# One of eight score slots per head moved from TensorE to VectorE and ScalarE in a decode attention kernel, with another slot map for the last head

## The chip, the cores and the metric

One core of one Trainium2 chip. The metric is the device time of one execution in microseconds (us).

## The reference, cut to what matters

Two attention blocks (A and B) for one query token, 32 heads each, 8192 cached keys and values of 128 numbers in bf16. The kernel walks through the 64 heads one after the other.

```python
q = (x @ wq).reshape(B, Sq, H, Dh).transpose(0, 2, 1, 3)          # 1 token, 32 heads
scores = jnp.einsum("bhqd,bhkd->bhqk", q, k_cache) * (Dh ** -0.5)  # 8192 scores per head
p = softmax(scores, axis=-1)
o = jnp.einsum("bhqk,bhkd->bhqd", p, v_cache)
return o.transpose(0, 2, 1, 3).reshape(B, Sq, H * Dh) @ wo
```

## The kernel before

K of one head lies in SBUF as 128 partitions by 64 columns of 128 numbers; the 64 columns are cut into 8 *slots* g0 to g7 of 8 columns. A slot's scores come in one of two ways, by a letter in a map:

- "P": TensorE transposes the 8 blocks, ScalarE copies them to SBUF, TensorE multiplies them by q (one-column products), and one ScalarE copy brings the scores to `ssb`.
- "D": VectorE runs 8 fused multiplies with an accumulator, straight from K.

What follows the scores is the same for every head: the max reduce on VectorE and GpSimd's max over the partitions, the exp on ScalarE, GpSimd's sum over the partitions, and on TensorE the *PV products* (probabilities times V), the *selection* (which picks out and adds up the parts of their result), and, after VectorE's normalisation, the *projection* by `wo`.

The lines that matter, with cuts:

```python
NK, NV, NWO, QB0, VCH, MAP = 4, 4, 8, 8, 4, "PDPDPDDD"
...
# GpSimd, for every head n
def armax(n):
    W(pl, s_rmx, n + 1)                                  # after VectorE's max reduce
    pl.partition_all_reduce(gmx[:, n:n+1], mx[:, n:n+1], 128, ROP.max).then_inc(s_g1, 1)
    W(pl, s_g1, n + 1)
    pl.tensor_scalar(nb[:, n:n+1], gmx[:, n:n+1], -scale, None, AluOpType.mult).then_inc(s_nbr, 1)
def aradd(n):
    W(pl, s_expd, n + 1)                                 # after ScalarE's exp
    pl.partition_all_reduce(gs[:, n:n+1], rs[:, n:n+1], 128, ROP.add).then_inc(s_gsr, 1)
...
# SyncE: K of head n may be loaded when head n-4 has been read
W(sp, s_tf, NP * m); W(sp, s_sttd, ND * m)
sp.dma_start(kb[:, n % NK], kvw[b][:, h]).then_inc(s_kl[n % NK], 16)
...
# VectorE, one turn per slot t = 8 n + g, in this order:
#   g1: max reduce of head n-1    g4: normalisation of head n-2
#   g5: reciprocal of head n-1 (waits for GpSimd's sum gs)    then the slot's own 8 multiplies
ins = dve.scalar_tensor_tensor(junk[...], kb[:, n % NK, j, :], 1.0, qrep[:, n % 2, :],
        AluOpType.mult, AluOpType.mult, accum_out=ssb[:, n % 2, cm[j]:cm[j] + 1])
```

## Time and profile before

| | before |
|---|---|
| time, first three executions | 1574.52 us median (1568.42 to 1582.11) |
| VectorE / TensorE / ScalarE busy | 38% / 26% / 12% |
| share of the 16 transfer engines | 46% |
| steady period, max reduce to max reduce | 24.26 us |

No engine is near full. Here are lines of the page of the kernel before: span, busy us (share) per engine, the K and V queue's packets, MB and share of the span, the chain of waits that ended last by what held it, and groups with count, busy us, mean ns of one, then the idle time before them and what ended it.

```profile
span 1571.5 us, 17156 instructions
PE 416.0 (26%) x4736; PEld 248.4 (16%) x4736; DVE 598.2 (38%) x5383; ACT 185.8 (12%) x513; POOL 67.3 (4%) x198
...
q1 hardware_dynamic: 30196, 285.23, 46.0%
...
issue 70%; DVE 22%; POOL 4%; ACT 1%; DMA 1%; POOLq 1%; PE 0%; ACTq 0%; SPq 0%; DVEq 0%
...
L467 DVE TENSOR_SCALAR oT<-sb,rinv 128x1 bf16<-128x1 f32 x64 | 14.1, 221 | 670.3 <-PE sb L341 670.1
...
L375 ACT ACTIVATE psb<-ssb,nb 128x64 bf16<-128x64 f32 x64 | 22.2, 348 | 1195.6 <-POOL nb L213 1195.6
...
L461 DVE RECIPROCAL rinv<-gs 128x1 f32<-128x1 f32 x64 | 10.5, 164 | 279.9 <-POOL gs L217 279.9
L213 POOL TENSOR_SCALAR nb<-gmx 128x1 f32<-128x1 f32 x64 | 16.7, 260 | 725.3 <-issue 725.3
L217 POOL PARTITION_ALL_REDUCE gs<-rs x64 | 25.7, 402 | 391.1 <-issue 391.1
```

Look at the last two lines. GpSimd itself computes for 17 us and 26 us, but stands 725 and 391 us in front of these instructions with "issue" as the reason: nothing that the profile counts as a wait. That "issue" is 70% of the chain. ScalarE's exp waits 1196 us for the first of them.

The timeline of the kernel before, over one loop of the middle (start, duration, engine, instruction; idle time before in brackets; the VectorE multiplies are among the lines left out):

```profile
810.97 0.22 DVE L456 TENSOR_REDUCE mx<-ssb 128x1 f32<-128x64 f32 x1
811.01 0.33 SPq L153 DMA_DIRECT2D kb<-in_B_k_cache_dram  x1
...
811.29 0.38 POOL L211 PARTITION_ALL_REDUCE gmx<-mx  x1 [5.64 <-DVE mx L456]
811.38 0.43 SPq L166 DMA_DIRECT2D vb<-in_B_v_cache_dram  x1
...
822.33 0.26 POOL L213 TENSOR_SCALAR nb<-gmx 128x1 f32<-128x1 f32 x1 [10.67 <-issue]
822.63 0.35 ACT L375 ACTIVATE psb<-ssb,nb 128x64 bf16<-128x64 f32 x1 [18.27 <-POOL nb L213]
...
824.74 0.22 DVE L467 TENSOR_SCALAR oT<-sb,rinv 128x1 bf16<-128x1 f32 x1 [9.95 <-PE sb L341]
...
828.57 0.40 POOL L217 PARTITION_ALL_REDUCE gs<-rs  x1 [5.97 <-issue]
...
829.00 0.16 DVE L461 RECIPROCAL rinv<-gs 128x1 f32<-128x1 f32 x1 [4.04 <-POOL gs L217]
```

This is the loop that sets the time. Max reduce, then about 11 us until GpSimd's scaled maximum `nb`, then the exp, then about 6 us until GpSimd's sum `gs`, then VectorE's reciprocal; behind it, in VectorE's order, stand slots g5 to g7 and the next max reduce. I call the stretch from the end of the max reduce to the start of `nb` **the step**.

Two stretches of the kernel before, of about the same kind (the columns are the stretch and its length, busy us and instructions of PE, PEld, DVE, ACT and POOL, granted TensorE clock, transfer share, GB/s): the step of head 32, and that of head 62, near the end, when all K and V are loaded.

```profile
811.00:823.00 12.00, 0.00 (x0) 0.00 (x0) 3.79 (x34) 0.37 (x3) 0.64 (x2) 0.50 0.91 357
1533.70:1541.10 7.40, 0.00 (x0) 0.00 (x0) 3.43 (x32) 0.00 (x0) 0.38 (x1) 0.50 0.00 0
```

VectorE does about the same in both (3.79 and 3.43 us); the transfers run in one only, and the step is 4 to 5 us shorter without them.

### The profile page before, as it was taken

To read this page: it belongs to the slowest core of one execution; us is meant where nothing else is said; L and a number is where in the kernel's file an instruction comes from. 1 tells how busy PE (TensorE), PEld (TensorE's weight loads), DVE (VectorE), ACT (ScalarE), POOL (GpSimd) and SP (SyncE) were. 2 spreads that over 40 slices of the span, in tenths; PEclk is the share of its full clock that TensorE was granted. 3 is DMA by queue.
4 is the path that set the end of the run, shared out by engine and by line. 5 is a ranking of instruction groups with operands and counts; after the bars stand their busy time and mean duration, and the time that the engine had idled before them with its cause. 6 is when DMAs were issued, how large, how long until landed. Compare 5 with 4: busy or idle time off the path is not lost.

```text
span 1571.5 us, 17156 instructions
## 1 busy us (share of the span) xinstructions
PE 416.0 (26%) x4736; PEld 248.4 (16%) x4736; DVE 598.2 (38%) x5383; ACT 185.8 (12%) x513; POOL 67.3 (4%) x198
## 2 busy tenths in 40 slices
PE   2313133132231331322312223132232221331321
PEld 2101122121111110111111111011111110111110
DVE  3243342442433424424334243342442433424343
ACT  1101101011011010110110101011011010110110
POOL 0000000000000000000000000000000000000000
PEclk9955555555555555555555555555555555555555
DMA  9953544535435345354353443534535435345400
GB/s 380 424 216 131 221 158 175 217 127 209 179 153 220 152 180 217 123 213 172 160 221 143 188 191 140 220 133 199 198 140 215 178 154 221 135 197 209 158 22 0
DMA packets 30291, 286.32 MB, mean 182 GB/s; under 512 B 4210, under 2 KB 12404, under 8 KB 12916
## 3 DMA queue, kind: packets, MB, share of 16 engines
q1 hardware_dynamic: 30196, 285.23, 46.0%
q8 instruction: 38, 0.62, 0.2%
q14 instruction: 57, 0.47, 0.1%
HBM read 285.21 MB, written 0.00 MB: 181 GB/s over the span
## 4 chain that ended last, share of the span: by engine, by line
issue 70%; DVE 22%; POOL 4%; ACT 1%; DMA 1%; POOLq 1%; PE 0%; ACTq 0%; SPq 0%; DVEq 0%
DVE junk L440 21%; POOL gs L217 2%; POOL gmx L211 2%; POOL nb L213 1%; DVE mx L456 1%; ACT psb L375 1%; DMA wqs<-in_A_wq_dram 1%; DVE rinv L461 1%; POOLq L59 0%; POOLq L213 0%; PE qpb L229 0%; ACTq L123 0%; DVE osb L474 0%; SPq L144 0%; PE misc L354 0%
## 5 line engine op out<-in xcount | busy, mean ns | idle before, releaser
L440 DVE SCALAR_TENSOR_TENSOR junk<-kb,qrep 128x128 bf16<-128x128 bf16 x2560 | 557.7, 286 | 1.0 <-ACT qrep L368 0.8
L295 PE MATMUL sb<-qT,kt 128*128 128x1 bf16 x1536 | 73.9, 169 | 1093.0 <-ACT kt L392 1093.0
L467 DVE TENSOR_SCALAR oT<-sb,rinv 128x1 bf16<-128x1 f32 x64 | 14.1, 221 | 670.3 <-PE sb L341 670.1
L295 PEld LDWEIGHTS sb<-qT,kt 128*128 128x128 bf16 x1536 | 67.4, 109 | 1107.3 <-ACT kt L392 1107.0
L440 DVE DVE_READ_ACCUMULATOR junk<-kb,qrep 128x1 f32 x2560 | 209.4, 82 | 0.1
L279 PE MATMUL tb<-ident,kb 128*128 128x128 bf16 x1536 | 185.8, 297 | 2.2 <-DMA kb<-in_A_k_cache_dram 2.2
L375 ACT ACTIVATE psb<-ssb,nb 128x64 bf16<-128x64 f32 x64 | 22.2, 348 | 1195.6 <-POOL nb L213 1195.6
L279 PEld LDWEIGHTS tb<-ident,kb 128*128 128x128 bf16 x1536 | 139.6, 135 | 102.0 <-issue 99.6
L321 PE MATMUL db<-vb,psb 128*4 128x512 bf16 x1024 | 149.6, 574 | 16.7 <-ACT psb L375 16.7
L392 ACT ACTIVATE kt<-tb 128x512 f32<-128x512 f32 x192 | 113.2, 590 | 110.7 <-PE tb L279 110.7
L461 DVE RECIPROCAL rinv<-gs 128x1 f32<-128x1 f32 x64 | 10.5, 164 | 279.9 <-POOL gs L217 279.9
L213 POOL TENSOR_SCALAR nb<-gmx 128x1 f32<-128x1 f32 x64 | 16.7, 260 | 725.3 <-issue 725.3
L217 POOL PARTITION_ALL_REDUCE gs<-rs x64 | 25.7, 402 | 391.1 <-issue 391.1
L354 PE MATMUL misc<-wos,oT 128*1 128x512 bf16 x64 | 40.3, 630 | 2.8 <-DVE oT L467 2.8
L211 POOL PARTITION_ALL_REDUCE gmx<-mx x64 | 24.2, 379 | 375.8 <-DVE mx L456 375.8
L385 ACT ACTIVATE dsb<-db 128x512 bf16<-128x512 f32 x64 | 37.5, 586 | 2.2 <-PE db L321 2.2
L321 PEld LDWEIGHTS db<-vb,psb 128*4 128x4 bf16 x1024 | 23.3, 80 | 33.4 <-ACT psb L375 17.7
L368 ACT ACTIVATE qrep<-sb 128x128 bf16<-128x128 f32 x64 | 17.8, 278 | 69.6 <-PE sb L254 69.6
L254 PE MATMUL sb<-diag,ones 128*128 128x128 bf16 x64 | 16.9, 264 | 22.7 <-issue 22.0
L341 PE MATMUL sb<-sel,dsb 128*128 128x1 bf16 x256 | 17.0, 170 | 0.7 <-ACT dsb L385 0.7
L341 PEld LDWEIGHTS sb<-sel,dsb 128*128 128x128 bf16 x256 | 11.8, 107 | 29.2 <-ACT dsb L385 28.8
L423 DVE TENSOR_SCALAR diag<-ident,qT 128x128 bf16<-128x128 bf16 x64 | 16.0, 250 | 0.1
(20 smaller groups left out, 70.7 us busy)
## 6 DMA issues: line engine op xcount, KB each, us to landing
kb<-in_A_k_cache_dram SPq DMA_DIRECT2D x32, 2048.0 KB, 8.0
vb<-in_A_v_cache_dram SPq DMA_DIRECT2D x32, 2048.0 KB, 12.7
kb<-in_B_k_cache_dram SPq DMA_DIRECT2D x32, 2048.0 KB, 7.7
vb<-in_B_v_cache_dram SPq DMA_DIRECT2D x31, 2048.0 KB, 12.4
wqs<-in_A_wq_dram SPq DMA_DIRECT2D x1, 4096.0 KB, 13.2
wos<-in_A_wo_dram SPq DMA_DIRECT2D x32, 128.0 KB, 12.5
wqs<-in_B_wq_dram SPq DMA_DIRECT2D x1, 4096.0 KB, 42.6
wos<-in_B_wo_dram SPq DMA_DIRECT2D x32, 128.0 KB, 12.2
```

The costliest lines, as they stand in the source:

```text
L211: pl.partition_all_reduce(gmx[:, n:n + 1], mx[:, n:n + 1], 128, ROP.max).then_inc(s_g1, 1)
L213: pl.tensor_scalar(nb[:, n:n + 1], gmx[:, n:n + 1], -scale, None, AluOpType.mult).then_inc(s_nbr, 1)
L217: pl.partition_all_reduce(gs[:, n:n + 1], rs[:, n:n + 1], 128, ROP.add).then_inc(s_gsr, 1)
L279: ins = pe.transpose(tb[E % 2][:, i * 128:(i + 1) * 128], kb[:, n % NK, j, :], ident[:, :])
L295: ins = pe.matmul(sbk[n2 % 2][:, cm[j]:cm[j] + 1], kt[:, E % 2, i * 128:(i + 1) * 128], qT[:, n2:n2 + 1], start=True, stop=True,)
L321: ins = pe.matmul(dbk[n3 % 2][32 * c:32 * c + 4, 0:512], psb[:, n3 % 2, c0:c0 + 4], vb[:, n3 % NV, 4 * i:4 * i + 4, :].rearrange("p a d -> ...
L341: ins = pe.matmul(sbk[(n4 + 1) % 2][:, OC:OC + 1], dsb[:, n4 % 2, m * 128:(m + 1) * 128], sel[:, m:m + 1], start=(m == 0), stop=(m == 3),)
L354: pe.matmul(misc[0:1, 0:DO], oT[:, n5:n5 + 1], wos[:, n5 % NWO, :], start=(h == 0), stop=(h == H - 1),).then_inc(s_pjd, 1)
L375: act.activation(psb[:, n6 % 2, :], ssb[:, n6 % 2, :], AF.Exp, bias=nb[:, n6:n6 + 1], scale=scale, accum_out=rs[:, n6:n6 + 1],).then_inc(s ...
L385: act.activation(dsb[:, n7 % 2, :], dbk[n7 % 2][:, :], AF.Copy).then_inc(s_devd, 1)
L392: act.activation(kt[:, E % 2, :].bitcast(F32), tb[E % 2][:, :].bitcast(F32), AF.Copy,).then_inc(s_ev, 1)
L440: ins = dve.scalar_tensor_tensor(junk[:, (Sd % 2) * 8 + i, :], kb[:, n % NK, j, :], 1.0, qrep[:, n % 2, :], AluOpType.mult, AluOpType.mult ...
```

## The change

The intent: take one of three slots from TensorE (g4), give it to VectorE as one 128x1024 multiply with 8 accumulating copies on ScalarE behind it ("A"), and in the last head give more slots to TensorE, so that the end of the program is shorter. TensorE's selection and projection also move ahead of the PV products.

```diff
-    NK, NV, NWO, QB0, VCH, MAP = 4, 4, 8, 8, 4, "PDPDPDDD"
+    NK, NV, NWO, QB0, VCH = 4, 4, 8, 8, 4
+    MAP, MAPL, NLAST = "PDPDADDD", "PDPDPAPD", 1
 ...
+        junk2 = SB("junk2", [128, 8, 128], BF)
+        prod = SB("prod", [128, 2, 8, 128], BF)
 ...  (TensorE: the block of PV products now stands behind selection and projection)
 ...  (ScalarE)
+                if 0 <= n < N and g >= 1 and smap(n)[g - 1] == "A":
+                    W(act, s_pm, A + 1)
 ...
+                    for i in range(8):
+                        ins = act.activation(
+                            junk2[:, i, :], prod[:, A % 2, i, :], AF.Copy,
+                            accum_out=ssb[:, n % 2, cm[j]:cm[j] + 1],
+                        )
+                    ins.then_inc(s_aacc, 1)
 ...  (VectorE, max reduce)
+                    W(dve, s_aacc, cumA[n1 + 1])
 ...  (VectorE, slot "A")
+                    dve.tensor_tensor(
+                        prod[:, A % 2], kb[:, n % NK, 8 * g:8 * g + 8, :], qrep_b(n, 8), AluOpType.mult,
+                    ).then_inc(s_pm, 1)
```

(The rest of the diff counts semaphores per head, because the maps now differ between heads.)

More of the change, by code (lines that the diff above doesn't have):

```diff
@@ L37, in bass_concat_heads__mha_block_cached__gqa_block_cached__decode_kernel, with smap, slots, colmap @@
     assert DO <= 512 and N <= 64 and JT == 64 and NG == 8
-    assert len(MAP) == NG and set(MAP) <= set("PD")
-    pslots = [g for g in range(NG) if MAP[g] == "P"]
-    dslots = [g for g in range(NG) if MAP[g] == "D"]
-    NP = len(pslots)
-    ND = len(dslots)
-    assert pslots == [2 * i for i in range(NP)] and NP >= 1 and ND >= 1
-    cm = {}
-    for i, g in enumerate(pslots + dslots):
-        for r in range(8):
-            cm[8 * g + r] = 8 * i + r
+    assert len(MAP) == NG and len(MAPL) == NG
+    def smap(n):
+        return MAPL if n >= N - NLAST else MAP
+    def slots(n, kind):
+        return [g for g in range(NG) if smap(n)[g] == kind]
+    for m_ in (MAP, MAPL):
+        pl_ = [g for g in range(NG) if m_[g] == "P"]
+        assert pl_ == [2 * i for i in range(len(pl_))] and len(pl_) >= 1
+        assert len([g for g in m_ if g == "A"]) <= 3 and len([g for g in m_ if g == "D"]) >= 1
+    def colmap(n):
+        cm = {}
+        c = 0
+        for kind in "PAD":
+            for g in slots(n, kind):
+                for r in range(8):
+                    cm[8 * g + r] = c
+                    c += 1
+        return cm
+    colmaps = [colmap(n) for n in range(N)]
+    NP_ = [len(slots(n, "P")) for n in range(N)]
+    NA_ = [len(slots(n, "A")) for n in range(N)]
+    ND_ = [len(slots(n, "D")) for n in range(N)]
+    cumP = [sum(NP_[:n]) for n in range(N + 1)]
+    cumA = [sum(NA_[:n]) for n in range(N + 1)]
+    cumD = [sum(ND_[:n]) for n in range(N + 1)]
     kvw = [b[1][0].rearrange("h (p j) d -> p h j d", p=128) for b in branches]
@@ L109, in bass_concat_heads__mha_block_cached__gqa_block_cached__decode_kernel @@
         s_dgr = SEM("s_dgr"); s_qrm = SEM("s_qrm"); s_qre = SEM("s_qre")
-        s_sttd = SEM("s_sttd"); s_scp = SEM("s_scp")
+        s_sttd = SEM("s_sttd"); s_scp = SEM("s_scp"); s_pm = SEM("s_pm"); s_aacc = SEM("s_aacc")
         s_rmx = SEM("s_rmx"); s_g1 = SEM("s_g1"); s_nbr = SEM("s_nbr")
@@ L126, in br_of, with qrep_b @@
             return n // H, n % H
+        def qrep_b(n, g8):
+            return qrep[:, n % 2, :].unsqueeze(1).broadcast_to([128, g8, 128])
         ST_RMAX = NG + 1
@@ L150, in dma_k @@
                     m = n - NK + 1
-                    W(sp, s_tf, NP * m)
-                    W(sp, s_sttd, ND * m)
+                    W(sp, s_tf, cumP[m])
+                    W(sp, s_sttd, cumD[m])
+                    W(sp, s_pm, cumA[m])
                 sp.dma_start(kb[:, n % NK], kvw[b][:, h]).then_inc(s_kl[n % NK], 16)
@@ L269, in _ @@
                     qrep_mm((t - ST_QREP) // NG)
-                if 0 <= n < N and MAP[g] == "P":
+                if 0 <= n < N and g % 2 == 0 and g // 2 < NP_[n]:
                     e = g // 2
-                    E = NP * n + e
+                    E = cumP[n] + e
                     if e == 0:
@@ L282, in _ @@
                 n2, g2 = t2 // NG, t2 % NG
-                if 0 <= n2 < N and MAP[g2] == "P":
+                if 0 <= n2 < N and g2 % 2 == 0 and g2 // 2 < NP_[n2]:
                     e = g2 // 2
-                    E = NP * n2 + e
+                    E = cumP[n2] + e
+                    cm = colmaps[n2]
                     if e == 0:
@@ L299, in _ @@
                     ins.then_inc(s_qkd, 1)
-                tp = t - ST_PV
-                if tp >= 0 and tp // NG < N and (tp % NG) % 2 == 0:
-                    n3 = tp // NG
-                    bt = (tp % NG) // 2
-                    if bt == 0:
-                        if n3 < 2:
-                            W(pe, s_dz, 2)
-                        W(pe, s_expd, n3 + 1)
-                        if n3 >= 2:
-                            W(pe, s_devd, n3 - 1)
-                    if n3 == N - 1 and VCH > 1:
-                        nbt = JT // 16
-                        need = ((bt + 1) * VCH + nbt - 1) // nbt
-                        prev = 0 if bt == 0 else (bt * VCH + nbt - 1) // nbt
-                        for c in range(prev, need):
-                            W(pe, s_vlc[c], 16)
-                    elif bt == 0:
-                        W(pe, s_vl[n3 % NV], 16 * (n3 // NV + 1))
-                    for c in range(4):
-                        i = 4 * bt + c
-                        c0 = cm[4 * i]
-                        ins = pe.matmul(
-                            dbk[n3 % 2][32 * c:32 * c + 4, 0:512],
-                            psb[:, n3 % 2, c0:c0 + 4],
-                            vb[:, n3 % NV, 4 * i:4 * i + 4, :].rearrange("p a d -> p (a d)"),
-                            start=(bt == 0), stop=(bt == JT // 16 - 1),
-                            tile_position=(0, 32 * c),
-                        )
-                    if bt == JT // 16 - 1:
-                        ins.then_inc(s_pvd, 1)
                 ts = t - ST_SEL
@@ L357, in _ @@
                     ).then_inc(s_pjd, 1)
+                tp = t - ST_PV
+                if tp >= 0 and tp // NG < N and (tp % NG) % 2 == 0:
+                    n3 = tp // NG
+                    bt = (tp % NG) // 2
+                    cm = colmaps[n3]
+                    if bt == 0:
+                        if n3 < 2:
+                            W(pe, s_dz, 2)
+                        W(pe, s_expd, n3 + 1)
+                        if n3 >= 2:
+                            W(pe, s_devd, n3 - 1)
+                    if n3 == N - 1 and VCH > 1:
+                        nbt = JT // 16
+                        need = ((bt + 1) * VCH + nbt - 1) // nbt
+                        prev = 0 if bt == 0 else (bt * VCH + nbt - 1) // nbt
+                        for c in range(prev, need):
+                            W(pe, s_vlc[c], 16)
+                    elif bt == 0:
+                        W(pe, s_vl[n3 % NV], 16 * (n3 // NV + 1))
+                    for c in range(4):
+                        i = 4 * bt + c
+                        c0 = cm[4 * i]
+                        ins = pe.matmul(
+                            dbk[n3 % 2][32 * c:32 * c + 4, 0:512],
+                            psb[:, n3 % 2, c0:c0 + 4],
+                            vb[:, n3 % NV, 4 * i:4 * i + 4, :].rearrange("p a d -> p (a d)"),
+                            start=(bt == 0), stop=(bt == JT // 16 - 1),
+                            tile_position=(0, 32 * c),
+                        )
+                    if bt == JT // 16 - 1:
+                        ins.then_inc(s_pvd, 1)
         @block.scalar
@@ L366, in _ @@
                     if m >= 2:
-                        W(act, s_sttd, ND * (m - 1))
+                        W(act, s_sttd, cumD[m - 1])
+                        W(act, s_pm, cumA[m - 1])
                     act.activation(qrep[:, m % 2, :], sbk[m % 2][:, QC:QC + 128], AF.Copy).then_inc(s_qre, 1)
@@ L385, in _ @@
                     act.activation(dsb[:, n7 % 2, :], dbk[n7 % 2][:, :], AF.Copy).then_inc(s_devd, 1)
-                if 0 <= n < N and MAP[g] == "P":
+                if 0 <= n < N and g % 2 == 0 and g // 2 < NP_[n]:
                     e = g // 2
-                    E = NP * n + e
+                    E = cumP[n] + e
                     W(act, s_tf, E + 1)
@@ L394, in _ @@
                     ).then_inc(s_ev, 1)
+                if 0 <= n < N and g >= 1 and smap(n)[g - 1] == "A":
+                    cm = colmaps[n]
+                    ga = g - 1
+                    A = cumA[n] + slots(n, "A").index(ga)
+                    W(act, s_pm, A + 1)
+                    if n >= 2:
+                        W(act, s_expd, n - 1)
+                    if A >= 1:
+                        W(act, s_aacc, A)
+                    for i in range(8):
+                        j = 8 * ga + i
+                        ins = act.activation(
+                            junk2[:, i, :], prod[:, A % 2, i, :], AF.Copy,
+                            accum_out=ssb[:, n % 2, cm[j]:cm[j] + 1],
+                        )
+                    ins.then_inc(s_aacc, 1)
                 for n8 in (n, n - 1):
-                    if 0 <= n8 < N and t == NG * n8 + 2 * NP + 1:
-                        W(act, s_qkd, NP * (n8 + 1))
-                        act.activation(ssb[:, n8 % 2, 0:8 * NP], sbk[n8 % 2][:, 0:8 * NP], AF.Copy).then_inc(s_scp, 1)
+                    if 0 <= n8 < N and t == NG * n8 + 2 * NP_[n8] + 1:
+                        W(act, s_qkd, cumP[n8 + 1])
+                        npt = 8 * NP_[n8]
+                        act.activation(ssb[:, n8 % 2, 0:npt], sbk[n8 % 2][:, 0:npt], AF.Copy).then_inc(s_scp, 1)
         @block.vector
@@ L427, in dve_slot @@
             def dve_slot(n, g):
-                idv = dslots.index(g)
+                cm = colmaps[n]
+                idv = slots(n, "D").index(g)
                 if True:
-                    Sd = ND * n + idv
+                    Sd = cumD[n] + idv
                     if idv == 0:
@@ L453, in _ @@
                     n1 = tr // NG
-                    W(dve, s_sttd, ND * (n1 + 1))
+                    W(dve, s_sttd, cumD[n1 + 1])
                     W(dve, s_scp, n1 + 1)
+                    W(dve, s_aacc, cumA[n1 + 1])
                     dve.tensor_reduce(mx[:, n1:n1 + 1], ssb[:, n1 % 2, :], AX.X, AluOpType.max).then_inc(s_rmx, 1)
@@ L474, in _ @@
                         dve.tensor_copy(osb[0:1, b, :], misc[0:1, 0:DO]).then_inc(s_accd, 1)
-                if 0 <= n < N and MAP[g] == "D":
+                if 0 <= n < N and smap(n)[g] == "D":
                     dve_slot(n, g)
+                if 0 <= n < N and smap(n)[g] == "A":
+                    A = cumA[n] + slots(n, "A").index(g)
+                    W(dve, s_kl[n % NK], 16 * (n // NK + 1))
+                    W(dve, s_qre, n + 1)
+                    if A >= 2:
+                        W(dve, s_aacc, A - 1)
+                    dve.tensor_tensor(
+                        prod[:, A % 2], kb[:, n % NK, 8 * g:8 * g + 8, :], qrep_b(n, 8), AluOpType.mult,
+                    ).then_inc(s_pm, 1)
 _INS = ['A_x', 'A_k_cache', 'A_v_cache', 'A_wq', 'A_wo', 'B_x', 'B_k_cache', 'B_v_cache', 'B_wq', 'B_wo']
```

## The prediction

> **What bounds the kernel.** Not a busy engine: VectorE is 38% busy, TensorE 26%, the transfers 46% (busy table, queue table). The timeline shows a loop of dependent steps, once per head, 64 times; in its steady part about 24.2 us from max reduce to max reduce:
> - max reduce on VectorE to GpSimd's scaled maximum: about 12.0 us;
> - to the exp on ScalarE: 0.3 us;
> - exp to the reciprocal on VectorE, which waits for GpSimd's sum: about 6.4 us;
> - reciprocal, three VectorE slots (g5, g6, g7: 24 fused multiplies, 0.213 us start to start), next max reduce: 5.50 us, always.
>
> So GpSimd's two reductions are 18 of 24 us. VectorE's slots g1 and g3 run under the 12 us; then it idles about 10 us to the normalisation and 4 us more to the reciprocal (wait table: 670 and 280 us in all). ScalarE waits 1196 us for the scaled maximum.
>
> The 12.0 us seems to hang on the K and V transfers, issued within 0.5 us of the max reduce and moving about 340 GB/s until the exp: in the last three heads, without transfers, the step is 7.4 to 8.0 us. VectorE does not matter there: head 62 has 31 VectorE operations in it (7.42 us), head 63 none (7.87 us).
>
> **What the change does.** Slots g1, g3, g5, g6, g7 stay "D". Only g4 turns from TensorE to the mixed kind, for 63 heads.
> - Removed per head: 8 transposes (1.03 us), 8 one-column products (0.4 us), one copy (0.6 us), all off the loop.
> - Added on VectorE: one 128x1024 multiply. The Trainium skill, "VectorE: DVE Perf Modes", section on the perf-mode tiers, gives a bf16 tensor_tensor two elements per cycle; estimate from its example: 0.7 us (1.2 if unpacked). It stands ahead of the reciprocal, which waits 4 us: hidden.
> - Added on ScalarE: 8 accumulating copies. The exp with its accumulator read takes 0.34 us start to next start, a 128x128 copy 0.28; estimate 0.35 to 0.5 us each, 3 to 4 us. They end about 6 to 7 us after the exp; the max reduce that needs them comes at 11.8. Hidden.
> - Selection and projection moved ahead of the PV products: normalisation 0.6 us earlier, into VectorE's wait. Nothing.
> - K loads still wait last for VectorE's slot g7, so the transfers collide with the same GpSimd step.
> - Ends: head 0, VectorE-bound, gets the multiply: +0.7 us. Last head: reciprocal to max reduce shrinks from 5.5 to about 4.5 us: -1 us. Sum about 0.
>
> **On the critical path:** practically nothing. Predicted **1574 us**, range **1561 to 1589** (the three runs of before span 1568 to 1582). Chances: faster by over 2% 0.03, within 2% 0.92, slower by over 2% 0.05.
>
> **What would show each step.** The period stays at 24.2 us with 12.0 / 0.3 / 6.4 / 5.5; the multiply begins about 2.5 us after the exp and VectorE's wait for GpSimd's sum shrinks by its length; ScalarE's busy time grows by 63 times 2.5 us or more while its wait for the scaled maximum stays near 1190 us; TensorE's busy time falls by about 85 us; the max reduce never waits for ScalarE.
>
> **What would make it wrong.** (a) "SBUF — State Buffer", section Who interferes with whom, says that a VectorE operation with two SBUF inputs contends with a GpSimd instruction that reads SBUF: the multiply falls into the sum step and could lengthen 6.4 us by up to 0.7 (45 us in all). Heads 62 and 63 speak against it. (b) The copies take over 1 us each and delay the max reduce. (c) GpSimd's step under the transfers changes length; each 0.5 us is 2%.

## More of the kernel before

What does GpSimd do in the step? The raw records of the trace, which the timeline leaves out because they are not counted as work, show it. For head 33, in us after the end of the max reduce:

```
 0.10  PARTITION_ALL_REDUCE gmx<-mx    its semaphore (which nb waits for) rises at 0.49
 0.42  MODIFY_POOL_CONFIG  (two, the last at 0.46)
12.71  TENSOR_SCALAR nb<-gmx
13.28  MODIFY_POOL_CONFIG  (two)
18.97  PARTITION_ALL_REDUCE gs<-rs
```

So the all-reduce is done after half a microsecond. What takes the time is the change of GpSimd's program between an all-reduce and a plain multiply, twice per head: 11.6 us under transfers, and 5.7 us for the way back (means over heads 3 to 59, last reconfiguration record to next operation).

The Trainium skill has a mechanism, in "GPSIMD Engine Reference", section Instruction dispatch: a pool reconfiguration can bring new code in by DMA, and the first call to a freshly loaded kernel pays about 6 us (5.95 measured there).

## The result, and the profile after

| | before | after |
|---|---|---|
| time, median of executions (range) | 1572.41 us (1561.47 to 1582.11, 15) | 1553.6 us (1548.46 to 1560.8, 12) |
| ratio | | 0.988, 95% interval 0.9854 to 0.9906 |
| matmuls on TensorE | 4736 | 3744 |
| the step, heads 3 to 59 | 12.07 us | 11.74 us |
| start of `nb` to exp | 0.29 | 0.29 |
| exp to reciprocal | 6.41 | 6.44 |
| reciprocal to end of max reduce | 5.51 (last head 5.50) | 5.51 (last head 3.67) |

A ratio is the mean time of one kernel's fast runs over that of the other's of the same rounds, so it is not quite the ratio of the medians. The time lies 1.2% below before and below the predicted range, which began at 1561. The same lines of the page after:

```profile
span 1549.4 us, 16231 instructions
PE 353.9 (23%) x3744; PEld 183.1 (12%) x3744; DVE 633.0 (41%) x5415; ACT 295.2 (19%) x1475; POOL 67.3 (4%) x198
...
L515 DVE TENSOR_SCALAR oT<-sb,rinv 128x1 bf16<-128x1 f32 x64 | 14.2, 221 | 628.0 <-PE sb L338 627.9
L404 ACT ACTIVATE psb<-ssb,nb 128x64 bf16<-128x64 f32 x64 | 22.2, 348 | 1150.4 <-POOL nb L239 1150.4
...
L435 ACT ACTIVATE junk<-prod 128x128 bf16<-128x128 bf16 x512 | 149.7, 296 | 4.5 <-DVE prod L531 4.5
...
L509 DVE RECIPROCAL rinv<-gs 128x1 f32<-128x1 f32 x64 | 10.5, 164 | 263.8 <-POOL gs L243 263.8
...
L239 POOL TENSOR_SCALAR nb<-gmx 128x1 f32<-128x1 f32 x64 | 16.6, 260 | 704.5 <-issue 704.5
L531 DVE TENSOR_TENSOR prod<-kb,qrep 128x1024 bf16<-128x1024 bf16 x64 | 43.7, 682 | 0.5 <-issue 0.5
L243 POOL PARTITION_ALL_REDUCE gs<-rs x64 | 25.7, 401 | 391.4 <-issue 391.4
```

GpSimd's idle time ahead of the scaled maximum has fallen from 725.3 to 704.5 us; ahead of the sum it has not moved. The timeline after, over the loop of the same head:

```profile
802.58 0.22 DVE L504 TENSOR_REDUCE mx<-ssb 128x1 f32<-128x64 f32 x1
802.61 0.33 SPq L179 DMA_DIRECT2D kb<-in_B_k_cache_dram  x1
...
802.90 0.38 POOL L237 PARTITION_ALL_REDUCE gmx<-mx  x1 [5.64 <-DVE mx L504]
...
815.29 0.26 POOL L239 TENSOR_SCALAR nb<-gmx 128x1 f32<-128x1 f32 x1 [12.01 <-issue]
815.59 0.35 ACT L404 ACTIVATE psb<-ssb,nb 128x64 bf16<-128x64 f32 x1 [19.07 <-POOL nb L239]
...
817.36 0.22 DVE L515 TENSOR_SCALAR oT<-sb,rinv 128x1 bf16<-128x1 f32 x1 [10.88 <-PE sb L338]
817.49 0.68 DVE L531 TENSOR_TENSOR prod<-kb,qrep 128x1024 bf16<-128x1024 bf16 x1
...
818.28 0.30 ACT L435 ACTIVATE junk<-prod 128x128 bf16<-128x128 bf16 x1
...
820.56 0.19 ACT L435 ACTIVATION_READ_ACCUMULATOR junk<-prod 128x1 f32 x1
...
821.47 0.40 POOL L243 PARTITION_ALL_REDUCE gs<-rs  x1 [5.92 <-issue]
...
821.91 0.16 DVE L509 RECIPROCAL rinv<-gs 128x1 f32<-128x1 f32 x1 [3.73 <-POOL gs L243]
```

The new work lies where the prediction put it: between the exp and the reciprocal, done 5.1 us after the start of the exp in the mean, while the max reduce that needs it starts 11.7 us after. (One head's step says little: that of head 32 is longer here than in the kernel before. Steps scatter by 0.4 to 0.6 us from head to head, so only the mean over many heads counts.)

Where the 22.1 us between the two profiled executions went, by summing the stretches over all heads: the step 20.9 us less, the last head's reciprocal to max reduce 1.8 less, the start of head 0 0.4 more; all other stretches together 0.2 more. So nearly all of it is in GpSimd's step, which the change does not touch. The experiments ask why.

### The profile page after: what moved, and what is told of

The parts are those of the page before. It is cut to its first block, busy times and chain, and to the rows that moved or that the text cites. A ratio compares the mean times of both kernels' runs of the same rounds, so it can differ in the third digit from the quotient of the medians.

```text
span 1549.4 us, 16231 instructions
## 1 busy us (share of the span) xinstructions
PE 353.9 (23%) x3744; PEld 183.1 (12%) x3744; DVE 633.0 (41%) x5415; ACT 295.2 (19%) x1475; POOL 67.3 (4%) x198
## 4 chain that ended last, share of the span: by engine, by line
issue 70%; DVE 23%; POOL 4%; ACT 1%; DMA 1%; POOLq 1%; PE 0%; ACTq 0%; SPq 0%; DVEq 0%
DVE junk L487 21%; POOL gs L243 2%; POOL gmx L237 2%; POOL nb L239 1%; DVE mx L504 1%; ACT psb L404 1%; DMA wqs<-in_A_wq_dram 1%; DVE rinv L509 1%; POOLq L79 0%; POOLq L239 0%; PE qpb L255 0%; ACTq L145 0%; ACT junk L435 0%; DVE prod L531 0%; DVE osb L522 0%
## 5 line engine op out<-in xcount | busy, mean ns | idle before, releaser
L322 PE MATMUL sb<-qT,kt 128*128 128x1 bf16 x1040 | 47.0, 166 | 1150.6 <-ACT kt L421 1150.2
L322 PEld LDWEIGHTS sb<-qT,kt 128*128 128x128 bf16 x1040 | 38.3, 103 | 1184.2 <-ACT kt L421 1170.5
L377 PE MATMUL db<-vb,psb 128*4 128x512 bf16 x1024 | 169.8, 558 | 0.0
L435 ACT ACTIVATE junk<-prod 128x128 bf16<-128x128 bf16 x512 | 149.7, 296 | 4.5 <-DVE prod L531 4.5
L305 PE MATMUL tb<-ident,kb 128*128 128x128 bf16 x1040 | 127.8, 301 | 3.6 <-DMA kb<-in_A_k_cache_dram 3.6
L305 PEld LDWEIGHTS tb<-ident,kb 128*128 128x128 bf16 x1040 | 96.4, 137 | 80.4 <-issue 76.0
L435 ACT ACTIVATION_READ_ACCUMULATOR junk<-prod 128x1 f32 x512 | 96.7, 189 | 0.0
L421 ACT ACTIVATE kt<-tb 128x512 f32<-128x512 f32 x130 | 75.2, 578 | 3.3 <-PE tb L305 3.3
L239 POOL TENSOR_SCALAR nb<-gmx 128x1 f32<-128x1 f32 x64 | 16.6, 260 | 704.5 <-issue 704.5
L531 DVE TENSOR_TENSOR prod<-kb,qrep 128x1024 bf16<-128x1024 bf16 x64 | 43.7, 682 | 0.5 <-issue 0.5
L237 POOL PARTITION_ALL_REDUCE gmx<-mx x64 | 24.2, 379 | 374.2 <-DVE mx L504 374.2
```

The lines of the kernel that those rows point to most:

```text
L237: pl.partition_all_reduce(gmx[:, n:n + 1], mx[:, n:n + 1], 128, ROP.max).then_inc(s_g1, 1)
L305: ins = pe.transpose(tb[E % 2][:, i * 128:(i + 1) * 128], kb[:, n % NK, j, :], ident[:, :])
L322: ins = pe.matmul(sbk[n2 % 2][:, cm[j]:cm[j] + 1], kt[:, E % 2, i * 128:(i + 1) * 128], qT[:, n2:n2 + 1], start=True, stop=True,)
L377: ins = pe.matmul(dbk[n3 % 2][32 * c:32 * c + 4, 0:512], psb[:, n3 % 2, c0:c0 + 4], vb[:, n3 % NV, 4 * i:4 * i + 4, :].rearrange("p a d -> ...
L421: act.activation(kt[:, E % 2, :].bitcast(F32), tb[E % 2][:, :].bitcast(F32), AF.Copy,).then_inc(s_ev, 1)
L435: ins = act.activation(junk2[:, i, :], prod[:, A % 2, i, :], AF.Copy, accum_out=ssb[:, n % 2, cm[j]:cm[j] + 1],)
```

## The experiments

Theories at the start. **S**: slot g4 leaving TensorE (or its replacement) shortens the step. **A**: the new tiles and semaphores lie elsewhere. **O**: TensorE's new order. **B**, for the step itself: a fixed GpSimd cost plus a part that the K and V transfers add. A later one, **L**: the length of TensorE's program. Every step below is the mean of heads 3 to 59 of one profiled execution (standard error 0.04 to 0.09 us, from the scatter of the heads). The runs were made on three chips; the kernel before took 1572.7 to 1576.0 us (median) on each of them, beside the runs. In the code cuts, " ..." stands for lines left out, such as waits and semaphores.

### New tiles and semaphores alone (e1_place)

```diff
 (the kernel before)
+        junk2 = SB("junk2", [128, 8, 128], BF)
+        prod = SB("prod", [128, 2, 8, 128], BF)
         ssb = SB("ssb", [128, 2, JT], F32)
+        s_pm = SEM("s_pm"); s_aacc = SEM("s_aacc")
```

> The kernel before with the two new tiles and two new semaphores allocated and not used, so that every later tile lies at the changed kernel's addresses. Theory S (slot g4 leaving TensorE shortens GpSimd's step from max reduce to scaled maximum, 12.07 us before, 11.74 us after): same as before, ratio 0.998 to 1.002, step 12.0 to 12.15 us. Rival A (addresses or semaphore numbers): ratio about 0.989, step about 11.75 us. Rival O (order of TensorE's instructions): same as before.

Measured: ratio 1.0004 (0.9968 to 1.004), step 12.14 us. A falls.

### TensorE's order alone (e2_order)

Edit: in the kernel before, the block of PV products is moved behind selection and projection; nothing else.

> The kernel before with only the PV products moved behind selection and projection in TensorE's order. Theory S: same as before, ratio 0.998 to 1.002, step 12.0 to 12.15 us. Rival A: same as before. Rival O: ratio about 0.989, step about 11.75 us.

Measured: ratio 0.9997 (0.9965 to 1.0029), step 12.09 us. O falls.

### Slot g4 alone (e3_slot) and slot g4 as plain VectorE work (e4_dve)

```diff
 e3_slot: (the changed kernel, TensorE's old order)
-    MAP, MAPL, NLAST = "PDPDADDD", "PDPDPAPD", 1
+    MAP, MAPL, NLAST = "PDPDADDD", "PDPDPAPD", 0
 e4_dve: (the changed kernel)
-    MAP, MAPL, NLAST = "PDPDADDD", "PDPDPAPD", 1
+    MAP, MAPL, NLAST = "PDPDDDDD", "PDPDPAPD", 0
```

> The changed kernel with TensorE's old order and with the ordinary slot map in the last head too: slot g4 on VectorE and ScalarE in all 64 heads, nothing else. Theory S: ratio about 0.989 to 0.991, step about 11.75 us, exp to reciprocal 6.4 us, reciprocal to max reduce 5.50 us, the last head included. Rival A: the same ratio (the tiles are there). Rival O: ratio 1.000, step 12.07 us.

> The changed kernel with slot g4 as 8 fused multiplies on VectorE (no multiply-and-copy pair, no ScalarE work), TensorE's new order, ordinary map in the last head too. The 8 multiplies take about 1.7 us ahead of the reciprocal, in its wait of about 4 us. Theory S in the form that TensorE's missing third slot is what matters: ratio 0.988 to 0.992, step about 11.75 us. Theory S in the form that the added ScalarE or 1024-element VectorE work matters: ratio 1.000, step about 12.07 us. Rival A and rival O cannot be told apart here: about 0.99.

Measured: e3_slot ratio 0.9917 (0.9883 to 0.9951), step 11.96 us; its profiled execution, 1569.5 us, was the slowest of its six (1557.4 to 1569.5), so its step overstates (the median, 9.8 us less over 64 heads, would make it about 11.8: an estimate). e4_dve ratio 0.9879 (0.9845 to 0.9912), step 11.63 us, without any ScalarE work and without the last head's map. So the gain comes with the slot leaving TensorE, and not from where the slot goes to. At this point S looked right.

### No K and V transfers (nb_before, nb_after)

```diff
             def dma_k(n):
+                if n >= NK:
+                    return
             def dma_v(n):
+                if n >= NV:
+                    return
 (and the waits for the loads ask for the first load only; wrong results on purpose)
```

> The kernel before with K and V loaded for the first four heads only and reused after that: no transfers of 4 MB per head beside GpSimd's step. The result is wrong on purpose. Theory B (the step from max reduce to scaled maximum is a fixed GpSimd cost of about 7.6 us plus about 4.4 us that the K and V transfers add): step 7.5 to 7.8 us in all heads, period about 19.8 us, time about 64 x 19.8 + 40 = 1290 to 1320 us, ratio about 0.83. Rival (the step is long for another reason in the middle heads, and the last heads are short because they are last): step stays near 12 us, ratio above 0.97.

> The changed kernel with the same cut of K and V loads (wrong result on purpose). If the change's gain comes through the transfers' share of GpSimd's step: step equal to that of the other cut kernel within 0.1 us, and the two times differ only by the last head, about 2 us. If it comes through something else that slot g4 does to GpSimd: step shorter by about 0.3 us here too, times 20 us apart.

Measured: 1318.83 us (ratio 0.8371) and 1316.95 us (0.8361); steps 7.67 and 7.64 us. The group line of nb_before for the scaled maximum, whose idle time was 725.3 us in the kernel before:

```profile
L217 POOL TENSOR_SCALAR nb<-gmx 128x1 f32<-128x1 f32 x64 | 16.6, 260 | 469.8 <-issue 469.8
```

B holds: 4.4 of the 12.1 us of the step are added by the transfers that run beside it (12.07 less 7.67). And without them the change leaves the step alone: the two cut kernels differ by 1.9 us, which is the last head (1.8). The gain therefore lies in the part of GpSimd's step that the transfers add.

### One TensorE slot fewer still (p1), and TensorE's work put back (x1_pe)

```diff
 p1: (as e4_dve)
-    MAP = "PDPDDDDD"
+    MAP = "PDDDDDDD"
 x1_pe: (as e4_dve), TensorE
+                if 0 <= n < N and g == 4 and n != H - 2:
 ...
+                    for i in range(8):
+                        ins = pe.matmul(qpb[:, 128:256], kb[:, n % NK, 32 + i, :], ident[:, :], start=True, stop=True)
+                    ins.then_inc(s_dm, 1)
 ...  (SyncE's K load waits for s_dm too)
```

> As the run with slot g4 on VectorE, but with slot g2 on VectorE too: one TensorE slot in place of two, the slots after the reciprocal unchanged. If each TensorE slot taken away shortens GpSimd's step (dose): step 11.2 to 11.4 us, ratio 0.974 to 0.98. If it was only the third slot, or chance of a build: step 11.6 to 11.8, ratio 0.987 to 0.99.

> As the run with slot g4 on VectorE, with 8 more 128x128 matmuls of K on TensorE in slot g4, written to an unused part of a bank and used by nothing (62 of 63 heads): TensorE's matmuls of the third slot are back, without its copy on ScalarE and its one-column products. If the TensorE work or the number of its instructions lengthens GpSimd's step: step 12.0 to 12.15 us, ratio 0.998 to 1.002. If it is the ScalarE copy or the products: step about 11.65 us, ratio about 0.988.

Measured: p1 ratio 0.9889 (0.9855 to 0.9923), step 11.73 us: no further gain, so it is no dose. x1_pe ratio 1.0055 (1.0025 to 1.0086), step 12.26 us: the gain is gone. Step and ratio both lie above what was expected if TensorE's work matters (12.0 to 12.15, 0.998 to 1.002), and this kernel is 0.5% slower than the kernel before; what the last 0.2 us of the step are is not known. The TensorE instructions are what matters, not ScalarE's copy or the one-column products.

### Where the extra TensorE work stands (x5_start, x6_burst)

```diff
 x5_start: (as e4_dve), TensorE, first of all
 ...
+            for i in range(8 * (N - 2)):
+                pe.matmul(qpb[:, 128:256], ones[:, :], ident[:, :], start=True, stop=True)
 x6_burst: (as x1_pe)
+                    if n >= 1:
+                        W(pe, s_rmx, n)
```

> As the run with slot g4 on VectorE, with 496 more 128x128 matmuls on TensorE in one block at the very start, ahead of the first projection: TensorE's program is as long as with the 8 matmuls per head (which took the gain away), but each head runs as without them. If the length of TensorE's program or where it lies matters: step 12.1 to 12.3 us. If it matters when TensorE works within a head: step 11.6 to 11.75 us. The block itself costs about 20 to 50 us at the start, so read the step and the period, not the time.

> As the run with 8 more matmuls per head in slot g4, but held back until the max reduce of the head before is done, so that they run in the first microsecond of the K and V transfers and of GpSimd's step. If TensorE work near the start of that step is what lengthens it, by closeness in time: step 12.3 us or longer. If TensorE's work after the exp, ahead of the reciprocal, is what lengthens it (it no longer ends later): step 11.6 to 11.8 us.

Measured: x5_start step 12.11 us; its heads are those of e4_dve (11.63), and the 496 added matmuls all run ahead of them. x6_burst step 12.16 us, neither of the two numbers expected: held back to 0.1 us after the max reduce, just as the transfers begin, the matmuls do no more harm than anywhere else. So it is not when TensorE works. In x5_start nothing of a head was changed, and still the step went back; S, in the form "less TensorE work per head", falls. Theory L took its place.

### Longer or shorter programs (s1_pe_end, s2_short_before, s3_dve_end, s4_pe_longer)

```diff
 s1_pe_end: (as e4_dve), TensorE, last of all
 ...
+            for i in range(496):
+                pe.matmul(qpb[:, 128:256], ones[:, :], ident[:, :], start=True, stop=True)
 s2_short_before: (the kernel before, all three TensorE slots kept; wrong result on purpose)
-                    for i in range(8):          # one-column products of a slot
+                    for i in range(0, 8, 2):    # two-column products
 ...
-                    for c in range(4):          # PV products
+                    for c in range(3):
 s3_dve_end: (as e4_dve), VectorE, last of all
 ...
+            for i in range(992):
+                dve.memset(junk[:, i // 128, i % 128:i % 128 + 1], 0.0)
 s4_pe_longer: (the kernel before) 1024 matmuls as in s1_pe_end, last of all
```

> As the run with slot g4 on VectorE, with 496 matmuls more in one block at the very end of TensorE's program, behind the last projection: no head is touched, only the program is longer. If the length (or the place in memory) of TensorE's program sets GpSimd's step: step 12.05 to 12.3 us in heads that run before the block is ever reached. If the work itself mattered: step 11.6 to 11.75 us. The block adds some 55 us at the end, so read the step and the period, not the time.

> The kernel before, with three TensorE slots, their transposes and ScalarE copies kept, but with 16 matmuls per head fewer (4 two-column products in place of 8 one-column ones per slot, 12 PV products in place of 16): TensorE's program is then as long as in the run with slot g4 on VectorE (3712 matmuls). The result is wrong on purpose. If program length is the cause: step 11.6 to 11.8 us, ratio 0.986 to 0.992, though no slot was moved. If the third TensorE slot is the cause: step 12.0 to 12.15 us, ratio 0.998 to 1.002.

> As the run with slot g4 on VectorE, with 992 one-element memsets at the end of VectorE's program in place of anything on TensorE: the same number of instructions as the TensorE block. If only TensorE's program counts: step 11.6 to 11.75 us. If the total length of all programs counts: step 12.05 to 12.3 us. The block adds up to 60 us at the end.

> The kernel before with 1024 matmuls more at the end of TensorE's program (5760 in place of 4736). If longer programs mean a longer step without limit: step above 12.3 us. If there are two levels, by where things come to lie: step 12.0 to 12.2 us, or back at 11.7 us. The block adds some 115 us at the end.

Measured: s1_pe_end step 12.07 us, in heads that end long before the added block starts. s2_short_before step 11.73 us and ratio 0.9861 (0.9829 to 0.9893), the whole gain, with no slot moved. s3_dve_end step 11.78 us (0.03 above the range expected for "only TensorE's program counts", within its error of 0.08). s4_pe_longer 12.08 us: no longer than with 1024 matmuls fewer. The times of s1, s3 and s4 (ratios 1.0201, 1.0061, 1.0386) hold the added blocks. Taken off as the traces show them at the end (27.6, 28.5 and 57.7 us; an estimate), the medians of four executions each are 1573.7, 1552.4 and 1572.0 us. So the two levels show in the times too, and not only in one profiled step of each kernel. The scaled maximum's lines of s1_pe_end and s2_short_before, in that order (slot g4 is on VectorE in the first, on TensorE in the second):

```profile
L239 POOL TENSOR_SCALAR nb<-gmx 128x1 f32<-128x1 f32 x64 | 16.6, 260 | 723.0 <-issue 723.0
```

```profile
L213 POOL TENSOR_SCALAR nb<-gmx 128x1 f32<-128x1 f32 x64 | 16.6, 260 | 704.9 <-issue 704.9
```

All runs with K and V transfers and with the multiply on GpSimd, sorted by TensorE's matmuls (each has a weight load beside it):

| run | slots on TensorE | matmuls | step us | period us | ratio |
|---|---|---|---|---|---|
| p1 | 1 | 2688 | 11.73 | 24.05 | 0.989 |
| e4_dve | 2 | 3712 | 11.63 | 23.91 | 0.988 |
| s2_short_before | 3 | 3712 | 11.73 | 23.94 | 0.986 |
| s3_dve_end | 2 | 3712 | 11.78 | 23.97 | block |
| e3_slot | 2 | 3712 | 11.96 | 24.19 | 0.992 |
| the change | 2 | 3744 | 11.74 | 23.98 | 0.988 |
| x5_start | 2 | 4208 | 12.11 | 24.37 | block |
| s1_pe_end | 2 | 4208 | 12.07 | 24.28 | block |
| x1_pe | 2 | 4216 | 12.26 | 24.54 | 1.006 |
| x6_burst | 2 | 4216 | 12.16 | 24.40 | 1.002 |
| before | 3 | 4736 | 12.07 | 24.26 | 1 |
| e1_place | 3 | 4736 | 12.14 | 24.39 | 1.000 |
| e2_order | 3 | 4736 | 12.09 | 24.29 | 1.000 |
| s4_pe_longer | 3 | 5760 | 12.08 | 24.32 | block |

There are two levels, with the edge between 3744 and 4208 matmuls: the mean step is 11.72 us below it (without e3_slot) and 12.12 us above. Each level was seen on all three chips. A second mark in the packets of the trace goes with them without exception: the first 2% of a head's 4.3 MB have landed 2.04 to 2.15 us after the max reduce in the programs of 4208 matmuls and more, and 2.24 to 2.31 us after it in the shorter ones, although the K load is issued at the same moment (0.18 to 0.19 us before the end of the max reduce). Where the step is shorter, the first K packets come later.

What stays open: why the length acts. TensorE's instruction fetches (the instruction queue whose packet count goes with its matmuls) are not it directly: none of them falls into the step in any of the profiles looked at packet by packet (those of the table). One guess is that a longer program moves something in device memory, so that GpSimd's reconfiguration is held up more while K and V are read; no run tests it or shows the place of anything in memory.

### The step taken away (f1_nb_before, f2_nb_after)

If the reconfigurations are the loop, the one multiply by minus scale should not be on GpSimd.

```diff
 (the kernel before, and the changed kernel) GpSimd
-                W(pl, s_g1, n + 1)
-                pl.tensor_scalar(nb[:, n:n + 1], gmx[:, n:n + 1], -scale, None, AluOpType.mult).then_inc(s_nbr, 1)
 ...
 VectorE, one turn after the max reduce
+                    W(dve, s_g1, nn + 1)
+                    dve.tensor_scalar(nb[:, nn:nn + 1], gmx[:, nn:nn + 1], -scale, None, AluOpType.mult).then_inc(s_nbr, 1)
```

> The kernel before with the scaled maximum (the multiply by minus scale) computed on VectorE, after slot g1, in place of GpSimd, which then runs all-reduces only and is never reconfigured between them. If GpSimd's reconfigurations are the 12.0 and about 6 us of the loop: max reduce to exp falls to 2 to 3 us, exp to reciprocal to about 1.2 us, the loop to about 9 to 10 us, and transfers (4.3 MB per head at 340 to 400 GB/s, 11 to 13 us) become the limit: 780 to 880 us, ratio 0.50 to 0.56. If the all-reduce itself is the time: max reduce to exp stays over 10 us, ratio above 0.95.

> The changed kernel with the same move of the scaled maximum to VectorE. Ratio to before 0.50 to 0.56. Slot g4 is then off the limit (transfers), so this and the run of the kernel before with the same move should lie within 2% of each other.

Measured: 729.63 us (ratio 0.4633) and 729.53 us (0.463), both correct, and both below the ratios expected (0.50 to 0.56). The reconfiguration records fall from 260 to 4 in the whole run. Max reduce to `nb` takes 1.84 us in f1_nb_before (it includes slot g1), the period is 11.02 us, and the page of f1_nb_before shows what holds it now:

```profile
PE 414.7 (57%) x4736; PEld 257.1 (35%) x4736; DVE 596.1 (82%) x5447; ACT 195.6 (27%) x513; POOL 54.2 (7%) x134
...
q1 hardware_dynamic: 30196, 285.23, 95.3%
...
DMA 86%; DVE 7%; PE 6%; issue 1%; SPq 0%; ACT 0%; POOL 0%; ACTq 0%
```

The transfers' queue is busy 95.3% of the span and they are 86% of the chain of waits; "issue" is 1%, where it was 70%. The time came out below the 780 to 880 us expected: the transfers keep up 394 GB/s in the mean, the upper end of what I had allowed them, and 64 periods of 11 us are only some 705 us. The exp to reciprocal stretch is 3.5 us, not the 1.2 expected: VectorE has other work in its order ahead of the reciprocal (slot g3, and the normalisation, for which it waits 1.5 us in the mean on TensorE). Slot g4 is worth nothing here, as expected: the two lie within 0.1%.

## Why the prediction was right or wrong

- **The loop and its other stretches: right, but not what fills them.** "GpSimd's two reductions are 18 of 24 us" took the time for that of the reductions. They take 0.4 us each; the rest is the reconfiguration between them (260 records, 4 in f1_nb_before). Exp to reciprocal (6.41 to 6.44 us) and reciprocal to max reduce (5.51) did not move, and the new work stayed off the loop.
- **The step that failed is "On the critical path: practically nothing", in the term "The period stays at 24.2 us with 12.0 / 0.3 / 6.4 / 5.5".** The 12.0 was taken as fixed by the transfers, since the change touches neither them nor GpSimd. It measured 11.74: 20.9 us of the 22.1 between the profiles. The prediction named the place (point c of its last paragraph) and gave it no weight. The cause is not a move of work, but TensorE's shorter program: the same gain appears with all three slots kept (s2_short_before) and goes with a block at the end that no head sees (s1_pe_end, built on e4_dve; on the change itself the length was not put back). Why the length acts stays open.
- **The ends: sign right, size off.** Head 0 got 0.4 us (said 0.7), the last head lost 1.8 us (said 1).
- **The multiply: right.** 0.68 us against 0.7 estimated from "VectorE: DVE Perf Modes", perf-mode tiers: two elements per cycle. It begins 1.9 us after the exp in the mean, where 2.5 was said.
- **The copies: hidden as said, but cheaper.** A copy with its accumulator read takes 0.29 us start to start, not 0.35 to 0.5. "ScalarE: Activation LUTs", in What ACT_TABLE_LOAD costs, gives 186 ns + 0.833 ns per element with immediates, which makes an estimate of 293 ns for 128; the trace's 296 ns agree. It would have been the better estimate, though in part by luck: the page does not say what the accumulator read adds. With the removed copy of 0.6 us, ScalarE's busy time grew by 109 us and not by over 157.
- **TensorE's busy time fell by 62 us, not 85:** the PV products, in their new place, show 170 us in place of 150.
- **VectorE's wait for the sum** shrank by 0.25 us per head, not by the multiply's length: the normalisation came 0.35 us sooner (1.77 after 2.12 us behind the exp). The prediction named both effects, but did not take the one off the other. ScalarE's wait for the scaled maximum fell to 1150 us, where about 1190 was said: partly the shorter step, partly more ScalarE work ahead of it.
- **The feared contention did not come.** "SBUF — State Buffer", Who interferes with whom, has a VectorE operation with two SBUF inputs contend with a GpSimd instruction that reads SBUF. The stretch with the multiply in it grew by 0.03 us: GpSimd was being reconfigured then, and its all-reduce of 0.4 us came later.

## What to carry to other kernels

When an engine stands idle with "issue" as the reason, look at the records that are not counted as work: here a reconfiguration of GpSimd, twice per head, was 17 of 24 us (11.6 and 5.7), and moving one 128x1 multiply to another engine was worth 54% of the time, while the change under study, made around it, was worth 1%. A gain of 1% in a loop that waits on such a reconfiguration can come from the length of some other engine's program: before it is put down to the work that moved, keep the work and change only the length. Do not call a stretch fixed because the change does not touch it; give it a range from what it does in other parts of the trace.

## What the Trainium skill lacked or had wrong

- "GPSIMD Engine Reference", Instruction dispatch, has the reconfiguration (about 6 us); the runs show 5.7 us on the way to the all-reduce, 7.2 us on the way to the multiply without transfers, and 11.6 us with 4.3 MB of K and V in flight. That other transfers stretch it, by 4.4 us here, the page does not say.
- No page has it that the length of TensorE's program, with nothing else changed, shifts the step with such a reconfiguration under transfers by about 0.4 us (11.63 to 11.78 us up to 3744 matmuls, apart from 11.96 in the slowest execution of e3_slot; 12.07 to 12.26 us from 4208).
- "ScalarE: Activation LUTs" gives the cost of an ACTIVATE but not that of its accumulator read: 0.19 us as recorded, overlapped so that a pair of 128 elements takes 0.29 us start to start.
